# Rest rows of the first feed-forward product joined to the seven block products as prepared stacks

## The chip, the cores and the metric

The kernel runs on one core of one Trainium2 chip. The metric is device time in microseconds (us) of one execution. The engines are named as in the profile: PE (TensorE, matmuls), DVE (VectorE), ACT (ScalarE), POOL (GpSimd) and SP (SyncE, which issues most transfers); SPq and the like stand for the queue of instructions of an engine that only issues or waits.

## The reference

```python
x = A_x                                   # 1 x 2048 x 576
xn = layernorm(x)                         # no scale, no shift
qkv = xn @ wqkv                           # 32 heads of 18
phi = lambda t: where(t > 0, t + 1, exp(t)) + 1e-6
kv, z = sum over s of phi(k) v^T, phi(k)  # linear attention, not causal
o = (phi(q) @ kv) / (phi(q) . z + 1e-6)
s = o @ wo
h = gelu(xn @ w1 + b1)                    # w1: 576 x 4608
g = silu(h @ w2 + b2)                     # w2: 4608 x 576
out = x + s * g
```

## The kernel before

Every fp32 operand is split into a high and a low part (tiles ending in H and L, or h and l), and a product takes three matmuls: high by high, low by high, high by low. On top of that the large products use a seven-product scheme for 2x2 blocks (Winograd's form of Strassen's): sums of blocks are formed beforehand, seven block products are taken, and the results are combined.

The program has three stages, laid end to end on TensorE.

1. Keys and values (0 to about 155 us). Tiles of x are loaded, normalised, transposed and split (`x_hi`, `x_lo`, `x_sum`, `s_hi`, `s_lo`) into xH, xL, xSH and xSL, and these are also stored to DRAM (`x_dram`), since only half of the rows of x lie in SBUF at a time. Each has 4 column blocks of 128 rows and so many k slots.
2. Queries (about 155 to 282 us). Ten rounds r, with base = (8 + r) x 14 steps. A round runs a `Proj` (the query projection of a pair of 128-row tiles: psum tiles a, b, z, e; line 363) and two `Attend` halves. Attend transposes the queries scaled by the denominator (`pbuf`, transposed by PE into `ptp`, line 877; the last 64 columns of `pbuf` are filled by an ACT copy, line 869), casts them into `th` and multiplies them by the weights `kw` and `kr` (line 909). `kr` are copies of `kw` moved by some partitions with SBUF-to-SBUF transfers (lines 837 and 840). Beside it run the reloads of x (line 345), loads and sums of blocks of w2 (`w2r`, `w2o`, lines 491 to 525), and the stores of s (`s_dram`).
3. The feed-forward part (282 to 1071 us, and a tail to 1103). Two halves of x, nine chunks c of 512 hidden units each. A chunk is two `Up` steps (n counts them, 36 in all) and seven `product` calls of 24 matmuls each into the accumulators `macc`. An Up computes the first product for 256 hidden units and 512 rows: seven block products in the order UP = (1, 6, 7, 5, 2, 3, 4), all by the matmul at line 1162 with 512 columns. In the first half the operands of w1 are formed from `w1raw` (class W1: sums `T` on POOL, casts `hi` on ACT, subtractions `lo` on DVE) and stored in DRAM as `op_*`; in the second half W1Loaded reads them back.

D = 576 is 4 x 128 + 64. The 64 rest rows are a fifth k slot (KT = 5) that holds the high parts in one half of the partitions and the low parts in the other. In an Up two rest matmuls are added to each of the products 5, 2, 3 and 4, so these have 8 matmuls and the products 1, 6 and 7 have 6.

The order of the work on DVE, ACT, POOL and PE is that of the program text: `in_order` chains the instructions of each engine, and `add(step, what)` with `at_step(step)` puts work into the text at a numbered step. SP issues in the order of the text too. Each transfer on SP's queue uses one of eight completion semaphores in turn and so waits for the eighth one before it. `stage` takes one of six buffers; the tag `stw` has two.

Of the kernel before, what the change touches and what calls it, by code (L numbers as in the profile page):

```python
# [24 lines left out]
KT = 5  # L25
NF = F // P
# [11 lines left out]
NSP = 14  # L38
Q_ORDER = [4, 5, 6, 7, 0, 1, 2, 3]
# [3 lines left out]
def linear_attention_gated_ffn(ctx, tc, x, wqkv, wo, w1, b1, w2, b2, out):  # L43
# [40 lines left out]
    def stage_w1(name):  # L84
        return w1r.tile([P, 2 * KT * P], F32, tag="stw", name=name)

# [19 lines left out]
    b2b = pers.tile([P, D], F32, name="b2b")  # L106
# [14 lines left out]
    w1_dram, w2_dram = {}, {}  # L121

# [362 lines left out]
    def w2_load(c, pool, tag):  # L485
        src = w2_blocks(c)
        if tag == "wa":
            tiles = [pool.tile([P, KT * 2 * P], F32, tag=tag, name=f"w2r{c}{r}") for r in range(2)]
            parts = [t[:, : 2 * D].rearrange("p (n a d) -> p n a d", n=2, a=2) for t in tiles]
            for r in range(2):  # L490
                nc.sync.dma_start(parts[r], src[:, r])
        else:
            t = pool.tile([P, CF * D], F32, tag=tag, name=f"w2r{c}")
            nc.sync.dma_start(t, w2[c])
# [78 lines left out]
    x_raw(0, 0)  # L573
    wkq.split_k(3, kt_raw(raw_k, 3), GP)
# [16 lines left out]
    x_raw(0, 1)  # L591
    for i in (3, 2, 1, 5, 4):
        x_sum(0, i, GP, xf(0, 1))
# [9 lines left out]
    x_raw(1, 0)  # L603
    x_lo(1, 0)
# [6 lines left out]
    x_hi(1, 1), x_lo_tmp(1), x_lo(1, 1)  # L611
# [21 lines left out]
    def plan_pair(p):  # L633
        base = p * NSP
        def prepare(q, s, at_stats, at_norm, at_t, at_lo):
            add(base + at_stats, x_stats, q, s)
            add(base + at_norm, x_norm, q, s)
            if at_t is not None:
                add(base + at_t, transpose_x, q, s)
                add(base + at_t, x_hi, q, s)  # L640
                if s == 0:
                    add(base + at_lo, x_raw, q, s)
                add(base + at_lo, x_lo, q, s)
# [9 lines left out]
        if p == 1:  # L653
# [9 lines left out]
            add(base + 2, x_raw, 2, 0)  # L663
            add(base + 2, x_lo, 2, 0)
            add(base + 5, transpose_x, 2, 1)
            add(base + 5, x_hi, 2, 1)
            add(base + 5, x_lo, 2, 1)
# [11 lines left out]
        else:  # L679
# [6 lines left out]
            if p + 1 < NPAIR:  # L686
                q = p + 1
                add(base, x_norm, q, 1)
                add(base + 3, transpose_x, q, 1)
                add(base + 3, x_hi, q, 1)  # L690
                sums(q, (4, 4, 4, 6, 5), 7, 10, DV)
                add(base + 4, x_lo, q, 1)
                add(base + 6, x_lo_tmp, q)
# [61 lines left out]
    nc.sync.dma_start(b2b, bass.AP(tensor=b2.tensor, offset=b2.offset, ap=[[0, P], [1, D]]))  # L755
# [134 lines left out]

    class Attend:

        def __init__(self, r, s):
            self.t = t = pair_tile(Q_ORDER[r], s)
# [46 lines left out]
    class W1:  # L941


        def __init__(self, n):
            self.n = n
            raw = stage_w1(f"w1raw{n}")
            nc.sync.dma_start(raw, w1[n % NP])
            r4 = raw.rearrange("p (n k c) -> p n k c", n=2, k=KT)
# [4 lines left out]
        def T(self, i):  # L953
# [4 lines left out]
            if i in (5, 6):  # L958
                src[i] = w1p.tile([P, 2, P], F32, tag=f"w1t{i}", name=f"w1t{i}", bufs=1)
# [27 lines left out]
        def rest(self, n):  # L987
            return [v[:, (4, 2)[n]] for v in self.ops["ab"[n]]]

    W1_K = {"a": KT, "b": 3, 4: 2, 5: 2, 6: 2, 7: 2}  # L990

    class W1Loaded(W1):


        def __init__(self, n):
            self.n, self.ops = n, {}
            two = w1r.tile([P, 2, 2, 2, P], F32R, tag="stw", name=f"w67_{n}")
            for i in ("a", 6, 7, 5, "b", 4):
# [6 lines left out]
                nc.sync.dma_start(t.bitcast(F32), w1_dram[n % NP, i])  # L1005

# [8 lines left out]
    for r in range(NPAIR + 2):  # L1015
# [118 lines left out]
    gp = ctx.enter_context(tc.tile_pool(name="gp", bufs=1, side="right", reuse_waits="tile"))  # L1134
    fr = ctx.enter_context(tc.tile_pool(name="fr", bufs=1, side="right", reuse_waits="tile"))
    fl = ctx.enter_context(tc.tile_pool(name="fl", bufs=1, reuse_waits="tile"))

    macc = fl.tile([P, QH, 5, HD], F32, name="macc")
    C11, C12, C21, C22, U1 = range(5)
    mid = xp.tile([P, KT, 512], F32, tag="mid", name="mid")  # L1140
    m1_sb, u1_sb, u2_sb = (mid[:, i, :] for i in range(3))

    class Up:


        def __init__(self, n, w, xs):
            self.p, self.w = n % NP, w
            self.xb, self.xr = xs
# [5 lines left out]
        def mm(self, ps, i, rest=None, first=True):  # L1154
# [4 lines left out]
            if rest:  # L1159
                seq += [(v, self.xr[rest[1]]) for v in self.w.rest(rest[0])]  # L1160
# [12 lines left out]
        def step(self, i):  # L1173
# [12 lines left out]
            elif i == 5:  # L1186
                self.mm(E, 5, (1, 1))
                tt(B, E, u2_sb, op=ADD)  # L1188
                self.gelu(1, 1, B)
            elif i == 2:  # L1190
                self.mm(A, 2, (0, 0), first=False)
                self.gelu(0, 0, A)
            elif i == 3:
                self.mm(E, 3, (1, 2), first=False)
                tt(E, E, u1_sb, op=ADD)
                self.gelu(1, 0, E)
            else:
                self.mm(Y, 4, (0, 1))
# [43 lines left out]
    class HOps:  # L1242
# [11 lines left out]
        def S(self, i, pr):  # L1254
# [12 lines left out]
            else:  # L1267
                src[7, pr] = mid[:, 3 + pr, :]
# [20 lines left out]
    BIAS = {2: 0, 7: 1, 3: 1, 4: 0}  # L1289
    MINUS = (3, 5, 6, 7)  # L1290

    def product(c, i, q2, hs, w, held):
# [15 lines left out]
        if c > 0 or i in (5, 6):  # L1308
# [4 lines left out]
        elif i in BIAS:  # L1313
            h = BIAS[i]
            bb = b2b[:, None, h * HD : (h + 1) * HD].to_broadcast([P, 2, HD])
            if i in MINUS:
                nc.vector.tensor_tensor(dst, bb, src, op=SUB)
            else:
                nc.vector.tensor_tensor(dst, src, bb, op=ADD)
# [10 lines left out]
    tails = {}  # L1330

    def load_xs(t):
        F = lambda v: v.bitcast(F32)
        if t < 2:
            raw = stage_w1(f"xs{t}")
            xt, s_t = raw[:, :D], raw[:, KT * P : KT * P + D]
        elif t < 4:
            tiles = op_tile(w1p, [KT, P], "wa", 2, f"xs{t}")[1]
            xt, s_t = (F(v).rearrange("p a b -> p (a b)")[:, :D] for v in tiles)
# [116 lines left out]
    def x_swap(k):  # L1456
        _, a, b = X_PARTS[k]
        nc.sync.dma_start(x_tiles[k].bitcast(F32), x_dram[1][:, :, a:b])
# [46 lines left out]
    n_chunks = 2 * NC  # L1505
    for step in range(n_chunks):
# [3 lines left out]
        h = HOps(c)  # L1510
        if half == 0:
# [11 lines left out]
        if half == 0 and c < NC - 1:  # L1523
            add(base + 0, make, W1, w1t, 2 * step + 2)
            add(base + 4, make, W1, w1t, 2 * step + 3)
            add(base + 4, lambda n=2 * step + 2: plan_w1(add, w1t[n], base, **P0))
# [14 lines left out]
        elif not plain:  # L1541
            add(base + (14 if half == 0 else 7), make, W1Loaded, w1t, 2 * step + 2)
            swap = half == 0
            add(base + (22 if swap else 14), make, W1Loaded, w1t, 2 * step + 3)
            if step + 2 < n_chunks:
# [6 lines left out]
        if not plain:  # L1552
            if half == 0 and c == NC - 1:
                for k, at in ((2, 12), (3, 12), (1, 13), (0, 13)):
                    add(base + at, x_swap, k)
                add(base + 25, silu_first, C11)
# [87 lines left out]
```

## Time and profile before

| | |
|---|---|
| median of 3 runs | 1103.23 us (1102.82 to 1103.42) |
| span of the profiled execution, which is also its own time | 1103.0 us |
| PE busy | 1093.0 us in 6924 matmuls and transposes |
| DVE, ACT, POOL busy | 798.1, 505.7, 455.0 us |
| DMA moved | 271.92 MB, mean 247 GB/s |
| one chunk of the feed-forward part | two Ups of 11.33 us and 22.39 us of `product` |

A row of the timeline gives start and length in us, the engine, the line, the operation with out<-in, the shape, and in brackets the idle time ahead of it with what ended it. A row of the waits gives who waited at which line for whom: total us, times, longest. A row of the windows gives, for a stretch of time, its length, the busy us (and instructions) of PE, PEld (weight loads), DVE, ACT and POOL, the granted clock of PE, the DMA share (of 16 DMA engines) and GB/s.

### The profile page before, as it was taken

To read this page: it belongs to the slowest core of one execution; us is meant where nothing else is said; L and a number is where in the kernel's file an instruction comes from. 1 tells how busy PE (TensorE), PEld (TensorE's weight loads), DVE (VectorE), ACT (ScalarE), POOL (GpSimd) and SP (SyncE) were. 2 spreads that over 40 slices of the span, in tenths; PEclk is the share of its full clock that TensorE was granted. 3 is DMA by queue.
4 is the path that set the end of the run, shared out by engine and by line. 5 is a ranking of instruction groups with operands and counts; after the bars stand their busy time and mean duration, and the time that the engine had idled before them with its cause. 6 is when DMAs were issued, how large, how long until landed. Compare 5 with 4: busy or idle time off the path is not lost.

```text
span 1103.0 us, 18746 instructions
## 1 busy us (share of the span) xinstructions
PE 1093.0 (99%) x6924; PEld 1015.7 (92%) x6924; DVE 798.1 (72%) x1246; ACT 505.7 (46%) x916; POOL 455.0 (41%) x417
## 2 busy tenths in 40 slices
PE   8999999999999999999999999999999999999997
PEld 8999999999898998988989989899898998988987
DVE  5777567777687888978888788657475574664776
ACT  6766555545545444454444544524223233242352
POOL 5854434655446254453553633413324133342310
PEclk9999999999999999999999999999999999999999
DMA  5888837785988779688696789978666666766243
GB/s 205 308 264 280 275 116 226 256 286 190 350 282 314 262 237 369 182 299 300 219 369 194 267 285 376 371 236 281 212 220 205 219 200 210 229 197 223 85 139 124
DMA packets 95531, 271.92 MB, mean 247 GB/s; under 512 B 10381, under 2 KB 21133, under 8 KB 93391
## 3 DMA queue, kind: packets, MB, share of 16 engines
q1 hardware_dynamic: 90543, 260.68, 66.7%
q0 software_dynamic: 4896, 10.03, 5.5%
q8 instruction: 55, 0.90, 0.3%
q14 instruction: 37, 0.30, 0.1%
HBM read 165.94 MB, written 100.01 MB: 241 GB/s over the span
## 4 chain that ended last, share of the span: by engine, by line
PE 93%; DVE 2%; ACT 2%; issue 1%; DMA 0%; POOL 0%; SPq 0%; DVEq 0%; POOLq 0%; ACTq 0%
PE pm L1302 35%; PE e L1162 12%; PE zy L1162 10%; PE a L1162 10%; PE ps_s L909 5%; PE pl L419 5%; PE b L1162 4%; PE e L363 3%; PE a L363 2%; PE z L363 2%; PE pd L1427 2%; PE ps_kva L472 1%; PE b L363 1%; PE ptp L877 1%; PE pt L284 1%
## 5 line engine op out<-in xcount | busy, mean ns | idle before, releaser
L936 ACT CAST h_h<-g 128x512 fp32r<-128x512 f32 x204 | 120.1, 621 | 139.8 <-PE pm L1302 138.8
L939 DVE TENSOR_TENSOR h_l<-g,h_h 128x512 fp32r<-128x512 f32 x204 | 158.2, 775 | 0.0
L1310 DVE TENSOR_TENSOR macc<-macc,pm 128x576 f32<-128x576 f32 x128 | 96.3, 752 | 36.9 <-PE pm L1302 36.1
L1162 PE MATMUL a<-xH,wa 128*128 128x512 f32 x360 | 117.1, 390 | 0.0
L1269 POOL TENSOR_TENSOR mid<-g 128x512 f32<-128x512 f32 x34 | 45.4, 1336 | 108.2 <-ACT g L1170 108.1
L1312 DVE TENSOR_TENSOR macc<-pm,macc 128x576 f32<-128x576 f32 x90 | 68.2, 758 | 25.3 <-PE pm L1302 24.4
L1170 ACT ACTIVATE g<-b,b1c 128x512 f32<-128x512 f32 x36 | 24.9, 690 | 124.0 <-DVE b L1188 124.0
L1162 PEld LDWEIGHTS a<-xH,wa 128*128 128x128 f32 x360 | 67.6, 188 | 13.6
L1162 PE MATMUL e<-xSH,wb 128*128 128x512 f32 x216 | 66.6, 390 | 0.1
L1179 ACT COPY mid<-a 128x512 f32<-128x512 f32 x36 | 21.2, 588 | 90.8 <-PE a L1162 90.8
L1263 POOL TENSOR_TENSOR g<-g 128x512 f32<-128x512 f32 x34 | 51.4, 1512 | 17.1 <-DVE h_l L939 15.4
L1398 POOL TENSOR_TENSOR fin1l<-fin1h,fin1l 128x288 f32<-128x288 f32 x8 | 6.5, 808 | 121.7 <-DVE macc L1310 42.0
L1266 POOL TENSOR_TENSOR g<-g 128x512 f32<-128x512 f32 x34 | 52.5, 1543 | 10.0 <-DVE h_l L939 6.9
L1162 PE MATMUL a<-xL,wa 128*128 128x512 f32 x144 | 56.2, 390 | 0.0
L1182 DVE TENSOR_TENSOR mid<-b,mid 128x512 f32<-128x512 f32 x36 | 24.7, 687 | 36.3 <-PE b L1162 34.9
L1162 PE MATMUL b<-xSH,w 128*128 128x512 f32 x144 | 50.2, 389 | 0.0
L1162 PE MATMUL zy<-xSH,w 128*128 128x512 f32 x144 | 50.2, 389 | 0.0
L1162 PE MATMUL e<-xSH,w 128*128 128x512 f32 x144 | 50.2, 389 | 0.0
L1162 PE MATMUL zy<-xH,w 128*128 128x512 f32 x144 | 50.2, 389 | 0.0
L961 POOL TENSOR_TENSOR w1t<-w1raw 128x256 f32<-128x256 f32 x18 | 13.7, 762 | 86.3 <-DMA w1raw<-w 40.7
L1162 PEld LDWEIGHTS e<-xSH,wb 128*128 128x128 f32 x216 | 40.5, 188 | 9.0 <-DVE b L1188 0.6
L1260 POOL TENSOR_TENSOR g<-g 128x512 f32<-128x512 f32 x34 | 46.4, 1364 | 2.7
(931 smaller groups left out, 3579.0 us busy)
## 6 DMA issues: line engine op xcount, KB each, us to landing
op<-w SPq DMA_DIRECT2D x72, 256.0 KB
w<-op SPq DMA_DIRECT2D x72, 256.0 KB
w1raw<-w SPq DMA_DIRECT2D x18, 640.0 KB
w2raw<-w SPq DMA_DIRECT2D x10, 1152.0 KB
op_a<-wa SPq DMA_DIRECT2D x18, 640.0 KB
wa<-op_a SPq DMA_DIRECT2D x18, 640.0 KB
op<-w2o SPq DMA_DIRECT2D x19, 576.0 KB
w2r<-w SPq DMA_DIRECT2D x6, 1152.0 KB
```

The source lines that it names most:

```text
L363: nc.tensor.matmul(ps, st, mv, start=first and n == 0, stop=n == len(seq) - 1, skip_group_check=True,)
L419: nc.tensor.matmul(self.ps[n], st, self.wk(hl, k, n), start=(i == 0), stop=(i == n_all - 1))
L909: nc.tensor.matmul(self.ps[h], st[:, k, :], w[:, k, h * HD : (h + 1) * HD], start=(i == 0), stop=(i == len(self.seq) - 1),)
L936: nc.scalar.copy(pair[0], src)
L939: eng.tensor_tensor(pair[1], src, pair[0].bitcast(F32), op=SUB)
L1162: nc.tensor.matmul(ps.rearrange("p (c j) -> p c j", c=4), st, mv, start=first and n == 0, stop=n == len(seq) - 1, skip_group_check=True,)
L1260: tt(src[5, pr], A(1, 1), A(1, 0), op=SUB)
L1263: tt(src[6, pr], src[5, pr], A(0, 0), op=ADD)
L1266: tt(src[3, pr], src[6, pr], A(0, 1), op=SUB)
L1302: nc.tensor.matmul(ps[:, q, :HD], hs[p][st][:, cs], m[:, p, :], start=(n == 0 and i not in CHAIN), stop=(n == len(seq) - 1), skip_group_ch ...
L1310: nc.vector.tensor_tensor(dst, dst, src, op=SUB)
L1312: nc.vector.tensor_tensor(dst, src, dst, op=ADD)
```

## The change

The rest rows get one matmul in each of the seven products, so 42 + 7 matmuls in an Up in place of 42 + 8. For that, the block sums of the 64 rest rows (32 of each half of D's rest, RW = 32) are formed beforehand, and each is laid as a stack of four 32-row parts, high and low parts in such an order that one matmul over 128 rows gives all their products.

- In stage 1, `x_rest` copies the raw rest rows of x to DRAM (`xr_dram`), 4 small transfers for a pair of tiles, and one ACT copy `xr` for seven of the pairs.
- In stage 2, rounds r = 1 to 7 each make one `Rest`: (0, x), (0 to 4, w), (1, x). At `base` its input `rs` (128x512) is loaded on SP. At base + 3 ACT casts 128x384 (`hi(0)`), DVE subtracts (`lo(0)`) and SP issues four stores of 192 KB. At base + 4 POOL forms four sums of 128x128. At base + 6 the same follows for 128x512 (`hi(1)`, `lo(1)`, four stores of 256 KB). The stacks lie in DRAM as `xe_dram` and `we_dram`.
- In stage 3, each Up loads its stack of weights `we` (128x896, 448 KB). The seven stacks of x lie in three slots of xH and xSH that held the old rest rows (`load_x_over`) and in a new tile `x_extra` (1 MB), loaded at the start and again between the halves.
- w1 is loaded without its fifth k slot: `w1raw` and the operand a have 512 KB in place of 640, b has 256 in place of 384.
- The bias b2 is no longer read by `product`: `load_bias` loads it at the start of each half, and `set_bias` fills four of the accumulators with it by ACT copies of 128x4x288.
- The stores of s from the rounds r > 5 are issued by ACT in place of SP, and some small tiles move to other places.

The two tables of order show what stands where. First ACT at round r = 1, before: `scr<-a` are the drain and the first activation of the projection, `pbuf` are the copies that fill the last columns, `th` the cast of the transposed queries.

```order
L806 CAST kw_h<-kw_2045 128x576
L375 COPY scr<-a_2110 128x288
L387 ACTIVATE scr<-a_2110,c_84 128x288
L869 COPY pbuf_2040<-pbuf_2040 128x64
L884 CAST th_2174<-ptp_2168 128x640
L869 COPY pbuf_2041<-pbuf_2041 128x64
L806 CAST kw_h<-kr_2062 128x576
```

And ACT at the same place after the change (`re0True` is the stack of x, `rs0True` its input):

```order
L827 CAST kw_h<-kw_2098 128x576
L390 COPY scr<-a_2163 128x288
L923 CAST re0True_2204<-rs0True 128x384
L402 ACTIVATE scr<-a_2163,c_84 128x288
L890 COPY pbuf_2093<-pbuf_2093 128x64
L905 CAST th_2240<-ptp_2234 128x640
L890 COPY pbuf_2094<-pbuf_2094 128x64
L923 CAST re0True_2255<-rs0True 128x512
L827 CAST kw_h<-kr_2115 128x576
```

The two casts of the stack now stand between the drain of a and the cast of `kr`, the first of them ahead of the copy into `pbuf`.

SP at rounds r = 1 and 2, before:

```order
L840 DMA kr_2080<-kw_2045 120x576
L837 DMA kr_2080<-kw_2046 8x576
L345 DMA xL<-x_dram_100 128x768
L345 DMA xSH<-x_dram_100 128x1152
L345 DMA xSL<-x_dram_100 128x1024
L345 DMA xH<-x_dram_100 128x1024
L345 DMA xL<-x_dram_100 128x768
L491 DMA w2r_2219<-w 128x1152
L491 DMA w2r_2220<-w 128x1152
```

And after the change:

```order
L861 DMA kr_2133<-kw_2098 120x576
L858 DMA kr_2133<-kw_2099 8x576
L360 DMA xL<-x_dram_99 128x768
L360 DMA xSH<-x_dram_99 128x1152
L917 DMA rs0True<-xr_dram_102 128x512
L932 DMA xe_dram_104<-re0True_2204 128x384 x4
L932 DMA xe_dram_104<-re0True_2255 128x512 x4
L360 DMA xSL<-x_dram_99 128x1024
L360 DMA xH<-x_dram_99 128x1024
L360 DMA xL<-x_dram_99 128x768
L506 DMA w2r_2292<-w 128x1152
L506 DMA w2r_2293<-w 128x1152
```

The load of `rs` and the eight stores of the stacks stand ahead of the reload of xSL and of all that follows. The load of the next Rest stands behind the last of these rows.

SP at the start of stage 3, before (s is a store of the last Attend halves, `op` are stored operands of w1):

```order
L933 DMA op_5_3496<-w_0_3493 128x512
L918 DMA s_dram<-s_3528 128x576
L933 DMA op_b<-wb_3532 128x768
L933 DMA op_4_3540<-w_0_3537 128x512
L933 DMA op_a<-wa_3582 128x1280
L947 DMA w1raw_3587<-w 128x1280
```

And after the change (`we` are the stacks of weights for the first two Ups):

```order
L1217 DMA x_extra<-xe_dram_104 128x4x512
L985 DMA op_6_3680<-w_0_3677 128x512
L985 DMA op_7_3685<-w_0_3682 128x512
L985 DMA op_5_3690<-w_0_3687 128x512
L985 DMA op_b<-wb_3726 128x512
L985 DMA op_4_3734<-w_0_3731 128x512
L1044 DMA we_3758<-we_dram_106 128x896
L1044 DMA we_3760<-we_dram_106 128x896
L1235 DMA b2b<-b 128x576
```

The loads of `we` and b2b stand behind the stores of the last operands of the first Up, and `x_extra` ahead of four of them.

The diff, cut to its core:

```diff
+    def x_rest(p, s):
+        if s and p:
+            src = t1.tile([2 * RW, P], F32, tag="xr", name=f"xr{p}")
+            nc.scalar.copy(src, pts[p, 1][: 2 * RW, 4])
+        else:
+            src = xf(p, s)[: 2 * RW, 4]
+        dst = xr_dram[p // 4].rearrange("(r c) k j -> r c k j", c=4)[:, pair_cols(p)]
+        for k, at in enumerate(((0, 1), (3, 2))[s]):
+            nc.sync.dma_start(dst[:, at], src[k * RW : (k + 1) * RW])
...
+    class Rest:
+        def __init__(self, i, of_x=False):
+            self.i, self.of_x = i, of_x
+            self.s = stage(4 * P, f"rs{i}{of_x}").rearrange("p (k c) -> p k c", k=4)
+            nc.sync.dma_start(self.s, xr_dram[i] if of_x else w1e[i].rearrange("p (k c) -> p k c", k=4))
+        def hi(self, g):
+            n = (3, 4)[g]
+            t = w1r.tile([P, 2, 4, P], F32R, tag="stw", name=f"re{self.i}{self.of_x}{g}")
+            self.t = t[:, :, :n]
+            nc.scalar.copy(self.t[:, 0], self.s[:, :n])
+        def lo(self, g):
+            t, n = self.t, (3, 4)[g]
+            nc.vector.tensor_tensor(t[:, 1], self.s[:, :n], t[:, 0].bitcast(F32), op=SUB)
+            at = slice(3 * g, 3 * g + n)
+            for j in range(4):
+                v = t[:, j % 2 if self.of_x else j // 2].bitcast(F32)
+                dst = (xe_dram if self.of_x else we_dram)[self.i][RW * j : RW * (j + 1)]
+                nc.sync.dma_start(dst.rearrange("r c i j -> (r c) i j")[:, at], v)
+        def sums(self):
+            a, b, c, d = (self.s[:, k] for k in range(4))
+            tt = nc.gpsimd.tensor_tensor
+            if self.of_x:
+                tt(d, a, d, op=SUB), tt(c, c, d, op=SUB), tt(a, c, a, op=ADD), tt(b, b, c, op=SUB)
+            else:
+                tt(a, d, a, op=SUB), tt(d, c, d, op=SUB), tt(c, c, a, op=SUB), tt(b, b, c, op=SUB)
...
-            nc.sync.dma_start(s_dram[self.t], s_sb)
+            (nc.scalar if self.r > 5 else nc.sync).dma_start(s_dram[self.t], s_sb)
...
+        def load_rest(self):
+            n = self.n % NP
+            self.re = xe.tile([P, 7, P], F32R, tag="we", name=f"we{self.n}", bufs=2)
+            nc.sync.dma_start(self.re.bitcast(F32), we_dram[n // 4][:, n % 4])
...
+        if 1 <= r < NPAIR:
+            cur["re"] = None
+            i, of_x = ((0, True), (0, False), (1, False), (2, False), (3, False), (4, False), (1, True))[r - 1]
+            add(base, lambda i=i, of_x=of_x: cur.update(re=Rest(i, of_x)))
+            for g, at in ((0, 3), (1, 6)):
+                add(base + at, lambda g=g: cur["re"].hi(g))
+                add(base + at, lambda g=g: cur["re"].lo(g))
+            add(base + 4, lambda: cur["re"].sums())
+        if r == NPAIR - 1:
+            add(base + 8, load_x_over, 0)
...
+    load_x_extra(0)
+    for n in range(2):
+        w1t[n].load_rest()
...
+    def set_bias(s):
+        h = int(s in (C12, C22))
+        nc.scalar.copy(macc[:, :, s, :], tails["b2"][:, h : h + 1].to_broadcast([P, QH, HD]))
...
-            if rest:
-                seq += [(v, self.xr[rest[1]]) for v in self.w.rest(rest[0])]
+            seq += [(self.w.rest(i), xrest[i])]
...
+        if c == 0:
+            if half:
+                add(base + 2, load_bias)
+            for k, m in enumerate((C11, C22, C12, C21)):
+                add(base + (9 if half else 1) + k, set_bias, m)
```

More of the change, by code (lines that the diff above doesn't have):

```diff
@@ L25 @@
 KT = 5
+KM = 4
+RW = 32
 NF = F // P
@@ L121, in linear_attention_gated_ffn @@
     w1_dram, w2_dram = {}, {}
+    xr_dram = [dram.tile([P, 4, P], F32, name=f"xr_dram{i}") for i in range(2)]
+    xe_dram = [dram.tile([P, 4, 7, P], F32, name=f"xe_dram{i}") for i in range(2)]
+    we_dram = [dram.tile([P, 4, 7, P], F32, name=f"we_dram{i}") for i in range(NB4)]
     def x_operands():
@@ L487, in w2_load @@
         if tag == "wa":
-            tiles = [pool.tile([P, KT * 2 * P], F32, tag=tag, name=f"w2r{c}{r}") for r in range(2)]
-            parts = [t[:, : 2 * D].rearrange("p (n a d) -> p n a d", n=2, a=2) for t in tiles]
+            tiles = [pool.tile([P, 2 * D], F32, tag=tag, name=f"w2r{c}{r}") for r in range(2)]
+            parts = [t.rearrange("p (n a d) -> p n a d", n=2, a=2) for t in tiles]
             for r in range(2):
@@ L603, in linear_attention_gated_ffn @@
     x_raw(1, 0)
+    x_rest(1, 0)
     x_lo(1, 0)
@@ L1005, in __init__, with load_x_over @@
                 nc.sync.dma_start(t.bitcast(F32), w1_dram[n % NP, i])
+    X_OVER = {1: (xSH, 8, 0), 2: (xH, 7, 1), 4: (xH, 4, 2)}
+    X_EXTRA = (5, 3, 6, 7)
+    W_REST = {1: 0, 2: 1, 3: 2, 5: 3, 4: 4, 6: 5, 7: 6}
+    def load_x_over(i, which=(1, 2, 4)):
+        for k in which:
+            t, at, src = X_OVER[k]
+            nc.sync.dma_start(t[:, at].bitcast(F32), xe_dram[i][:, :, src])
     EW1 = nc.gpsimd
@@ L1544, in linear_attention_gated_ffn @@
             add(base + (22 if swap else 14), make, W1Loaded, w1t, 2 * step + 3)
+            for j in (2, 3):
+                add(base + (7, 14, 22)[j - 2 + swap], lambda n=2 * step + j: w1t[n].load_rest())
             if step + 2 < n_chunks:
```

101 lines of the change are left out of this document (63 added, 38 removed).

## The prediction

> **What bounds the kernel now.** I read the page first, then what TensorE waited for, then the chain that ended last, then the queues of SyncE and ScalarE around the places where the change adds work. The page:
>
> ```profile
> span 1103.0 us, 18746 instructions
> PE 1093.0 (99%) x6924; PEld 1015.7 (92%) x6924; DVE 798.1 (72%) x1246; ACT 505.7 (46%) x916; POOL 455.0 (41%) x417
> ```
>
> TensorE is busy for 99% of the span. What it waited for, first and last of six rows:
>
> ```profile
> PE warm L461 <- POOL ident masks.py:199: 1.7, 1, 1.7
> ...
> PE pt L284 <- DVE scr L324: 0.3, 1, 0.3
> ```
>
> No other wait of TensorE is longer than 0.6 us. So removed matmuls count in full, but every microsecond that TensorE is newly made to wait counts in full too; there is no slack on it. The chain of work (start, length, what) through a steady chunk gives the price of a matmul:
>
> ```profile
> 305.26 22.39 PE pm L1302 x168
> ...
> 329.04 1.37 PE b L1162 x6
> ...
> 331.77 1.81 PE e L1162 x8
> ```
>
> Products with 6 and with 8 matmuls stand side by side: 1.37/6 = 0.228, 1.81/8 = 0.226 us for one.
>
> **The gain.** An Up goes from 3x6 + 4x8 = 50 matmuls to 7x7 = 49. 36 Ups x 1 x 0.2265 us = **-8.2 us**, all on the path. The Trainium skill, "TensorE: Matmul & The Clock Gate", section "Back-to-back issue gap", gives some 131 ns as the sustained spacing of 512-wide matmuls; by that figure the gain would be an estimated 4.7 us. The rows disagree.
>
> **The cost at r=1 (the first Rest).** Rest(0, x) loads `rs` on SyncE's queue, and ScalarE casts it in `hi(0)`. In the new order that cast stands right behind `COPY scr<-a` and ahead of `ACTIVATE scr<-a,c`, of the pad `COPY pbuf` and of `CAST th` (the order is shown above). Its load takes the place that the reload of xSL had. Before, ScalarE's rows there are:
>
> ```profile
> 167.42 0.40 ACT L375 COPY scr<-a 128x288 f32<-128x288 f32 x1
> 171.04 0.50 ACT L387 ACTIVATE scr<-a,c 128x288 f32<-128x288 f32 x1 [3.23 <-PE a L363]
> 171.44 0.24 ACT L869 COPY pbuf<-pbuf 128x64 f32<-128x64 f32 x1
> 172.65 0.69 ACT L884 CAST th<-ptp 128x640 fp32r<-128x640 f32 x1 [0.97 <-PE ptp L877]
> ...
> 179.53 0.68 ACT L806 CAST kw_h<-kr 128x576 fp32r<-128x576 f32 x1 [0.63 <-DMA kr<-kw]
> 180.47 0.68 ACT L806 CAST kw_h<-kr 128x576 fp32r<-128x576 f32 x1 [0.26 <-DMA kr<-kw]
> ```
>
> SyncE's rows:
>
> ```profile
> 167.81 0.83 SPq L840 DMA_DIRECT2D kr<-kw  x1
> 168.74 0.67 SPq L837 DMA_DIRECT2D kr<-kw  x1
> 169.47 1.68 SPq L345 DMA_DIRECT2D xL<-x_dram  x1
> 171.21 0.41 SPq L345 DMA_DIRECT2D xSH<-x_dram  x1
> 171.67 0.65 SPq L345 DMA_DIRECT2D xSL<-x_dram  x1
> ...
> 191.99 0.40 SPq L494 DMA_DIRECT2D w2r<-w  x1
> ...
> 284.18 0.38 SPq L933 DMA_DIRECT2D op<-w  x1
> ```
>
> The shift copies `kr<-kw` issued at 165.8 to 168.7 release ScalarE only at 179.5 and 180.5, some 11 us after their issue. In windows (us; busy time of the five engines; granted clock; DMA share; GB/s):
>
> ```profile
> 10.00:15.00 5.00, 4.87 (x26) 4.80 (x26) 2.70 (x4) 3.09 (x8) 2.18 (x3) 0.66 1.04 391
> 160.00:172.00 12.00, 12.00 (x69) 9.54 (x68) 9.08 (x20) 6.64 (x15) 4.09 (x4) 1.00 0.24 56
> 176.00:178.00 2.00, 2.00 (x17) 1.99 (x16) 1.54 (x3) 1.84 (x4) 0.58 (x1) 1.00 1.03 312
> 178.00:180.00 2.00, 2.00 (x16) 1.85 (x14) 1.85 (x5) 1.37 (x3) 1.88 (x2) 1.00 0.59 192
> 182.00:184.00 2.00, 2.00 (x17) 2.00 (x17) 1.93 (x5) 0.00 (x0) 0.62 (x1) 1.00 1.02 419
> 182.00:265.00 83.00, 83.00 (x636) 83.00 (x636) 63.16 (x106) 43.80 (x89) 48.16 (x34) 1.00 0.66 238
> 282.00:304.00 22.00, 21.86 (x97) 17.75 (x97) 16.42 (x24) 14.31 (x27) 10.14 (x11) 1.00 0.97 340
> 663.00:688.00 25.00, 25.00 (x180) 24.50 (x179) 20.02 (x28) 10.45 (x16) 6.75 (x6) 1.00 0.96 373
> ```
>
> The queue runs dry until 172 (share 0.24), then is full while the copies are stuck in it, with a dip at 178 to 180. I take the queue as served in the order of issue: the last copy is done at 180.3, behind it xL (0.39 MB), xSH (0.59 MB) and the new load (0.26 MB), 1.24 MB at 419 GB/s = 3.0 us, so `rs` is there at 183.3. Then cast, ACTIVATE 0.50 and pad 0.24. The cast has 128x384 elements; rows of such size:
>
> ```profile
> L294 ACT CAST xH<-pt 128x384 fp32r<-128x384 f32 x8 | 3.8, 481 | 18.1 <-PE pt L284 18.1
> L327 ACT CAST xSH<-scr 128x1152 fp32r<-128x1152 f32 x8 | 9.2, 1145 | 1.5 <-POOL scr L324 1.5
> ```
>
> so the pad is ready at 183.3 + 0.48 + 0.50 + 0.24 less overlaps, about 184.4. The transposes `ptp` that read it start in these rows of TensorE:
>
> ```profile
> 171.90 0.71 PE L877 MATMUL ptp<-ident,pbuf 128*128 128x128 f32 x5
> ...
> 185.03 0.71 PE L877 MATMUL ptp<-ident,pbuf 128*128 128x128 f32 x5
> ...
> 200.21 0.71 PE L877 MATMUL ptp<-ident,pbuf 128*128 128x128 f32 x5
> ...
> 283.35 0.39 PE L1162 MATMUL b<-xSH,w 128*128 128x512 f32 x1
> ```
>
> 171.90 becomes 184.3: **+12.4 us**. Bounds: 5 us, if the load is only held up by bytes (rival 2), and 14 us.
>
> **r=2.** SyncE is in program order: eight stores of r=1's stacks (1.84 MB, the first ones only after the late cast), xSL, xH, xL (1.44 MB), two w2r (1.18 MB), then `rs` of Rest(0, w) (0.26 MB): 4.7 MB behind 183.8, 12.6 us at between 340 and 419 GB/s, so 196.4. The cast of it stands on ScalarE ahead of `ACTIVATE rt<-a,c`, and `lo(0)` stands on VectorE ahead of the last `kw_l<-kr`:
>
> ```profile
> 181.18 0.76 DVE L809 TENSOR_TENSOR kw_l<-kr,kw_h 128x576 fp32r<-128x576 f32 x1 [0.16 <-ACT kw_h L806]
> ```
>
> From that to the `ptp` at 185.03 were 3.85 us. 196.4 + 0.5 (cast) + 0.5 (lo) + 3.85 = 201.25, 16.2 us later than before: **+3.8 us** over r=1's. Bounds 0 and 6.
>
> **r=3 to r=6.** Each Rest moves 1.84 MB of stores and 0.26 MB of load in a period of 15.2 us (185.03 to 200.21), 138 GB/s on top of 238 at share 0.66; together 376 GB/s, a share of 1.04. The queue is full then. At r=3 `rs` is issued behind the w2r of 191.99 and its pad has to be cast some 1.2 us ahead of the `ptp` at 200.21, 6.6 us later. Ahead of it and in flight are w2r, xH and s (2.0 MB), with itself 5.4 us at 419 GB/s, in time; with the 1.84 MB of r=2's stores 9.8 us, 3.2 late. Between 0 and 3.2 for each of four, I take 2.0, since the stores of the step before are not all drained: **+8 us** (0 to 13). At r=7 only s and two `op` stores are ahead: 0.
>
> **What lies beside.** ScalarE's and VectorE's own work of Rest (casts of 0.48 and about 0.6, subtractions the same) and GpSimd's four sums hide in their idle time (VectorE 63 of 83 us, GpSimd 48 of 83). So do the `xr` copies and small stores of the first phase: TensorE's waits there are the six rows, and the x tiles wait for nothing of it. The last four stores of s on ScalarE's queue: 0. The smaller w1 loads and stores against the new `we` loads: +64 KB for an Up in the first half, 0.2 us of a queue: 0.
>
> **Start of the FFN.** we0 (0.46 MB) stands on SyncE behind `op_4`, which waits for VectorE and was issued at 284.18, and is read by the seventh matmul of the first Up, in the place of the row at 283.35. At 340 GB/s (share 0.97) its own bytes give 284.6 + 1.4 = 286.0, 2.6 us late; with x_extra (1.05 MB) and the six stores (1.8 MB) still ahead 11 us. I take **+5.5 us**, since part of these has left by then. The bias: four copies of 128x1152, 1.15 us each by the row of that size, on ScalarE, which wait for b2b behind we1. The chain there was already tight:
>
> ```profile
> 300.67 0.62 DVE b L1188
> 301.29 0.04 issue
> 301.33 2.11 PE e L1162 x8
> ```
>
> Between 0 (idle time of ScalarE, 7.7 of 22 us) and 4.6: **+2 us**. The exchange of x in the middle: 35 slots of 0.26 MB in place of 31, over a queue at share 0.96: 0 to 3, I take 0, since xL and the first half of xH now come with the same bytes ahead of them.
>
> **Clock.** The only long idle times of before are at the start; behind them a window of 5 us had 0.66 of the clock, 1.7 us lost. One stall of 12 us: **+1.5 us** (0 to 3).
>
> Sum: -8.2 + 12.4 + 3.8 + 8 + 5.5 + 2 + 1.5 = +25.0, against the profiled execution's 1103.0: **1128 us** (the median of the runs shown is 1103.23, 0.2 above it). A measurement of this kernel can tell 0.2%, 2.2 us, from no change.
>
> **Rivals.** 1. The forecast, 1119 to 1137 by its bounds taken together: 0.57.
> 2. The load passes the shift copies. Only bytes hold it up: 1.24 MB at 312 GB/s from 171.7 is 175.7, pad at 176.9, stall 5.0 in place of 12.4: 1121 us. For it: the dip at 178 to 180 shows that not all DMA engines are held by the copies. Against it: a load over 128 partitions needs all of them, and ScalarE saw the copies done in the order of their issue. 0.12. The Trainium skill, "DMA: Bandwidth & Descriptors", section "Queues, rings and completion order", speaks for it: completion is not first in, first out for an issuing engine; but each DMA engine takes descriptors in ring order, which speaks against it.
> 3. Only r=1 and r=2 cost: while TensorE stands 16 us the queue drains, and later loads are in time. -8.2 + 16.2 + 1.5 and 0 to 5 for the FFN's start: 1113 to 1118. 0.12.
> 4. Faster. `rs` lands before 171, so no cast holds the pad; then -8.2 and little else: 1095. It decides at the issue of that load: SyncE would have to be past xSH by about 168, while its rows show it held by the copies until 171.2. 0.10, for what I may have misread of the order.
> 5. The queue is full into the FFN: x_over, x_extra, we0, we1 and b2b are 3.5 MB, less 0.6 saved, 8.5 us at 340 GB/s, and w2's blocks are late for the products at 305; with 3 in the middle 1140. 0.06.
> Within 0.2%: between 4 and 3, 0.03.
>
> The range 1109 to 1142 leaves out rival 4, the no-change case and a few per cent at each end.
>
> **What would show it.** TensorE's `ptp` of r=1 with a wait of some 12 us put down to ScalarE's `pbuf`, and ScalarE's `re` cast waiting for the DMA `rs`; the same, smaller, at r=2 to 6; TensorE's first `L1262` row waiting for the DMA `we`; rows of seven matmuls at 1.59 us; the first Up starting at about 308 and the FFN from there to the end 8 us shorter. It is wrong if the wait of `rs` on ScalarE is under 2 us at r=1, or if the matmul spacing changes.

## The result, and the profile after

The changed kernel takes 1170.75 us (median of 5, 1167.0 to 1171.9), against 1103.33 us before: a ratio of 1.060 (95% interval 1.0588 to 1.0616). It is slower, as forecast, but by 67 us in place of 25. The profiled execution has a span of 1165.3 us, one of the faster ones. The page begins:

```profile
span 1165.3 us, 19017 instructions
PE 1106.0 (95%) x6888; PEld 1019.9 (88%) x6888; DVE 803.5 (69%) x1260; ACT 514.9 (44%) x945; POOL 461.9 (40%) x445
```

The 62.3 us between the spans split in two: TensorE's idle time went from 1103.0 - 1093.0 = 10.0 us to 1165.3 - 1106.0 = 59.3 us (+49.3), and its busy time rose by 13.0 us although 36 matmuls are gone. What TensorE waited for, the longest eight:

```profile
PE ptp L898 <- ACT pbuf L890: 20.4, 5, 11.3
PE a L1262 <- DMA we<-we_dram: 9.4, 1, 9.4
PE ptp L898 <- DVE th L910: 7.2, 4, 2.5
PE ps_s L961 <- DVE kw_l L830: 4.2, 1, 4.2
PE pm L1401 <- ACT h_h L988: 2.3, 1, 2.3
PE e L1262 <- DVE b L1288: 2.3, 1, 2.3
PE ptp L898 <- POOL pbuf L881: 1.8, 2, 1.0
PE warm L476 <- POOL ident masks.py:199: 1.7, 1, 1.7
```

Before, the last of these was the longest. ScalarE's own waits name what is behind the first row, the inputs of the Rests:

```profile
ACT re0True L923 <- DMA rs0True<-xr_dram: 14.9, 1, 14.9
...
ACT re3False L923 <- DMA rs3False<-w1e: 11.8, 1, 11.8
ACT re2False L923 <- DMA rs2False<-w1e: 11.6, 1, 11.6
ACT re4False L923 <- DMA rs4False<-w1e: 10.6, 1, 10.6
...
ACT re1False L923 <- DMA rs1False<-w1e: 8.6, 1, 8.6
...
ACT re0False L923 <- DMA rs0False<-w1e: 7.4, 1, 7.4
ACT re1True L923 <- DMA rs1True<-xr_dram: 6.3, 1, 6.3
```

All seven rounds are there. Round r = 1 on ScalarE reads as the prediction had it, cast, activation, pad, one behind the other:

```profile
181.31 0.51 ACT L923 CAST re0True<-rs0True 128x384 fp32r<-128x384 f32 x1 [14.89 <-DMA rs0True<-xr_dram]
181.72 0.49 ACT L402 ACTIVATE scr<-a,c 128x288 f32<-128x288 f32 x1
182.12 0.23 ACT L890 COPY pbuf<-pbuf 128x64 f32<-128x64 f32 x1
```

The later rounds, the start of the feed-forward part and the middle, on the chain that ended last:

```profile
190.12 7.98 DMA rs0False<-w1e
...
212.19 8.04 DMA rs1False<-w1e
...
235.47 7.33 DMA rs2False<-w1e
...
334.44 6.08 DMA we<-we_dram
...
757.62 9.29 DMA b2b<-b
...
797.19 1.62 PE a L1262 x7
800.42 1.61 PE zy L1262 x7
```

Each of these loads was needed about as soon as it was issued, or before, and each took 6 to 9 us to land.

**The clock.** Windows of the changed kernel around the first long wait (columns as before):

```profile
174.00:182.00 8.00, 0.00 (x0) 0.00 (x0) 0.15 (x1) 0.69 (x2) 0.45 (x1) 0.50 0.29 87
182.00:187.00 5.00, 4.60 (x21) 4.58 (x21) 3.92 (x8) 3.83 (x8) 1.33 (x3) 0.50 0.61 228
187.00:190.00 3.00, 3.00 (x25) 3.00 (x24) 2.42 (x6) 2.73 (x5) 1.76 (x2) 0.99 1.03 318
200.70:207.50 6.80, 5.94 (x27) 5.60 (x26) 4.37 (x10) 3.23 (x8) 4.07 (x6) 0.50 0.38 138
```

TensorE works again from 182.4, but at half its clock until 187, so 4.6 busy microseconds do the work of 2.3. At 200.7 the same follows a wait of only 4.2 us, and costs 3.0. The Trainium skill, "TensorE: Matmul & The Clock Gate", section "What's actually happening", has the clock halved after an idle window of some 3.4 us and restored after a busy one. The rows agree in part: the seven stretches at half clock last 3.4, 6.8, 10.2 or 13.7 us, multiples of that window, but the one from 200.7 was restored only after 6.8 us, 5.9 of them busy. Waits of 3.1 and 3.3 us in rounds 4 and 5 were enough here, and so were two of the four of 2.3 to 2.5 us.

### The profile page after: what moved, and what is told of

It reads as the page before. It is cut to its first block, busy times and chain, and to the rows that moved or that the text cites. A ratio compares the mean times of both kernels' runs of the same rounds, so it can differ in the third digit from the quotient of the medians.

```text
span 1165.3 us, 19017 instructions
## 1 busy us (share of the span) xinstructions
PE 1106.0 (95%) x6888; PEld 1019.9 (88%) x6888; DVE 803.5 (69%) x1260; ACT 514.9 (44%) x945; POOL 461.9 (40%) x445
## 4 chain that ended last, share of the span: by engine, by line
PE 79%; DMA 8%; DVE 4%; ACT 4%; issue 2%; POOL 2%; SPq 1%; DVEq 0%; ACTq 0%; POOLq 0%
PE pm L1401 33%; PE zy L1262 9%; PE e L1262 9%; PE a L1262 9%; PE b L1262 5%; PE pl L434 4%; PE pd L1516 2%; PE e L378 2%; PE a L378 1%; PE z L378 1%; PE ps_kva L487 1%; DMA rs0True<-xr_dram 1%; DMA b2b<-b 1%; DMA rs1False<-w1e 1%; DMA rs0False<-w1e 1%
## 5 line engine op out<-in xcount | busy, mean ns | idle before, releaser
L1409 DVE TENSOR_TENSOR macc<-macc,pm 128x576 f32<-128x576 f32 x136 | 102.2, 752 | 39.5 <-PE pm L1401 39.4
L1262 PE MATMUL a<-xH,wa 128*128 128x512 f32 x288 | 101.4, 393 | 0.0
L1411 DVE TENSOR_TENSOR macc<-pm,macc 128x576 f32<-128x576 f32 x98 | 74.2, 757 | 23.5 <-PE pm L1401 22.0
L1262 PEld LDWEIGHTS a<-xH,wa 128*128 128x128 f32 x288 | 54.0, 188 | 11.3
L1363 POOL TENSOR_TENSOR g<-g 128x512 f32<-128x512 f32 x34 | 49.5, 1457 | 27.5 <-DVE h_l L991 26.1
L1262 PE MATMUL e<-xSH,wb 128*128 128x512 f32 x144 | 50.4, 391 | 2.4 <-DVE b L1288 2.3
L1262 PE MATMUL e<-xSH,w 128*128 128x512 f32 x144 | 50.4, 390 | 0.0
L1015 POOL TENSOR_TENSOR mid<-w1raw 128x256 f32<-128x256 f32 x17 | 14.1, 832 | 81.1 <-DMA w1raw<-w 41.5
L1270 ACT ACTIVATE g<-e,b1c 128x512 f32<-128x512 f32 x36 | 24.8, 689 | 42.7 <-DVE e L1295 42.7
```

What stands on the lines that cost most here:

```text
L1262: nc.tensor.matmul(ps.rearrange("p (c j) -> p c j", c=4), st, mv, start=first and n == 0, stop=n == len(seq) - 1, skip_group_check=True,)
L1270: nc.scalar.activation(g, ps, AF.Gelu_apprx_tanh, bias=b1c[:, f : f + 1])
L1363: tt(src[6, pr], src[5, pr], A(0, 0), op=ADD)
L1409: nc.vector.tensor_tensor(dst, dst, src, op=SUB)
L1411: nc.vector.tensor_tensor(dst, src, dst, op=ADD)
```

## The experiments

Each ratio is to the kernel before, on the same chip.

**e1: the casts at the end of the round.**

```diff
-            for g, at in ((0, 3), (1, 6)):
+            for g, at in ((0, 9), (1, 12)):
...
-            add(base + 4, lambda: cur["re"].sums())
+            add(base + 10, lambda: cur["re"].sums())
```

> Only the places of the Rest steps in a round move: casts and subtractions from base + 3 and base + 6 to base + 9 and base + 12, the sums from base + 4 to base + 10; the loads stay. Theory A (an in-order ScalarE is held at the cast by a load that takes some 8 us to land): the casts now stand behind the pad copies and the load has landed, so most of the 35 us of TensorE waits in the rounds and the half clock behind them go: 1115 to 1130 us. Rival B (2.1 MB more in each round is more than the queue carries): the rounds stay long whatever the place, over 1150 us.

1153.65 us, 1.0454 (1.0436 to 1.0471): 17 us better, so the place counts, but over 1150 us, which is rival B's number. From round 2 on the rounds stay long, 16.8 to 20.9 us from one `ptp` to the next, where they took 15.2. The wait on the pad is gone from TensorE's list, and others are in its place:

```profile
PE z L378 <- ACT s L969: 10.9, 4, 3.4
PE a L378 <- ACT scr L390: 8.9, 1, 8.9
```

The second is round 1 again. That round has no Attend halves, so its last step comes right behind its projection, and the cast moved there still waits for the load:

```profile
182.83 0.51 ACT L923 CAST re0True<-rs0True 128x384 fp32r<-128x384 f32 x1 [5.81 <-DMA rs0True<-xr_dram]
```

The place of the cast chooses which work waits behind it.

**e2: the last stores of s back on SyncE.**

```diff
-            (nc.scalar if self.r > 5 else nc.sync).dma_start(s_dram[self.t], s_sb)
+            nc.sync.dma_start(s_dram[self.t], s_sb)
```

> The last stores of s go back from ScalarE's queue to SyncE's, nothing else. Theory A (the first we load waits for the store of s that took 7.7 us on ScalarE's queue, since it takes that store's memory): the 9.4 us wait of the first Up shrinks by 3 to 5 us, 1165 to 1168 us. Rival B (the load is late because the queue is full): unchanged within 2 us, 1169 to 1173 us.

1170.26 us, 1.0598 (1.0582 to 1.0614): unchanged. TensorE's wait for we is 9.8 us. The chain after had shown `we` behind a store of s of 7.7 us, and that was the last of several late things, not the cause. Theory A fell.

**e3: the second load of b2b early.**

```diff
-            if half:
-                add(base + 2, load_bias)
...
                 add(base + 13, load_x_over, 1, (2, 4))
+                add(base + 2, load_bias)
```

> The second load of b2b is issued in the last chunk of the first half, ahead of the exchange of x, in place of behind the stores of the first half's results. Theory A (ScalarE is held at the bias copy by that load): the 2.5 us of TensorE waits in the first chunk of the second half and the 3.4 us at half clock behind them go, 1166 to 1168 us. Rival B (the four copies of 1.15 us themselves are what delays the casts): 1170 to 1172 us.

1166.38 us, 1.0565 (1.055 to 1.0581): 4.4 us better, theory A. The late load of b2b, which held ScalarE and with it the casts for the first product of the second half, was most of the loss in the middle.

**e4: without Rest.** The rounds make no stacks; the feed-forward part loads as many bytes from the stored x.

```diff
-            add(base, lambda i=i, of_x=of_x: cur.update(re=Rest(i, of_x)))
-            for g, at in ((0, 3), (1, 6)):
-                add(base + at, lambda g=g: cur["re"].hi(g))
-                add(base + at, lambda g=g: cur["re"].lo(g))
-            add(base + 4, lambda: cur["re"].sums())
...
-            nc.sync.dma_start(self.re.bitcast(F32), we_dram[n // 4][:, n % 4])
+            nc.sync.dma_start(self.re.bitcast(F32), x_dram[0][:, n % 4, n % 24 : n % 24 + 7])
```

> The seven Rest steps are left out of the rounds; the feed-forward part loads stacks of the same size from the stored x instead, so its rest products are not those of the reference. Theory A (the rounds lose their time to Rest alone, 35 us of waits and the half clock behind them; the feed-forward part has its own losses at its start and its middle): rounds as before, 1103 - 4 for the matmuls + 9 to 18 for the start and the middle, 1108 to 1118 us. Rival B (the losses at the start of the feed-forward part also come from Rest's backlog): 1099 to 1104 us.

1114.27 us, 1.0093 (1.0078 to 1.0108): theory A. Rest costs 1170.75 - 1114.27 = 56 us. There was no wait for we at the first Up either: the order put that load at 275.27, some 7 us ahead of its use, where the changed kernel issues it at 334.44, after the first matmul of the Up at 329.68. So that wait went with Rest, in part as rival B has it; whether by the backlog or by the load's place ahead of the last stores of `op` in SyncE's queue, this run does not tell. What is left is 10 us above before.

```profile
ACT macc L1234 <- DMA b2b<-b: 6.2, 1, 6.2
```

That row is ScalarE's longest wait of the first chunk.

**e5: e1 with buffers of their own for the stacks.** (`tag="stw"` in w1r becomes `tag="re"`, two buffers in t2.)

> e1 (casts at the end of a round, 1153.7 us), and the stacks' tiles get two buffers of their own in place of sharing two with w2's operands. Theory A (in e1 the rounds are held by a ring: a cast of one waits until the store of the other has left its buffer, and the stores wait in the queue): another 10 to 25 us go, 1128 to 1144 us. Rival B (the volume of the queue sets the rounds): 1149 to 1154 us.

1151.41 us, 1.0434 (1.0416 to 1.0451): 2 us from e1. The shared ring was not the matter in e1; the time is rival B's.

**e6: e5 with each stack stored once.**

```diff
-            for j in range(4):
-                v = t[:, j % 2 if self.of_x else j // 2].bitcast(F32)
+            for j in range(2):
+                v = t[:, j].bitcast(F32)
```

> e5, and each stack's high and low parts are stored once in place of twice (0.92 MB in place of 1.84 in a round); the copies are made by the loads, which take 2 or 4 transfers over part of the partitions in place of one. Theory A (buffers and places were the whole matter): like e5 within 3 us. Rival B (the volume matters: 15.2 us of a round carry some 5.5 MB at 360 GB/s, the rounds before had 3.6): 6 to 15 us faster than e5.

1152.73 us, 1.0445 (1.0429 to 1.046): no gain as a whole, theory A's number. But the first Up started at 307.3 in place of e5's 313.8, so the rounds did gain 6.5 us from the smaller volume, as rival B has it. It was given back in the feed-forward part, where the loads are now two to four transfers each: TensorE's waits for we grew from 8.2 to 13.7 us, and the first chunk of the second half from 50.4 to 56.3 us.

**e7: the loads half a round earlier, the casts where they were.**

```diff
-            add(base, lambda i=i, of_x=of_x: cur.update(re=Rest(i, of_x)))
...
+            add(base, lambda: cur.update(re=cur["next"]))
+            if r < NPAIR - 1:
+                add(base + 5, lambda v=of[r]: cur.update(next=Rest(*v)))
```

> The changed kernel with the casts where they were, but the loads of the Rests of rounds 2 to 7 are issued in the middle of the round before. Theory A (a load of some 8 us issued too late holds ScalarE, and nothing else): rounds 2 to 7 lose their waits, only round 1's 11 us and its clock stay: 1130 to 1140 us. Rival B (ring of buffers and volume): the waits turn to others, 1150 to 1168 us.

1149.2 us, 1.0416 (1.04 to 1.0431): 21.5 us better, 0.8 us below rival B's range and far above theory A's. The pad waits of rounds 3 to 6 (9.1 us) and round 2's wait for `kw_l` (4.2 us) are gone and round 1's is left; the half clock between 200 and 300 is gone too.

```profile
PE ptp L898 <- ACT pbuf L890: 11.2, 1, 11.2
PE a L1266 <- DMA we<-we_dram: 8.7, 1, 8.7
PE ptp L898 <- DVE th L910: 6.5, 6, 1.3
```

So late loads are a large part of the rounds, but not all.

**e9: all of it.** The first load goes ahead of the shift copies, with e7's early loads at base + 7, e6's single stores, own buffers for the inputs and the second cast, and e3's early b2b.

> The changed kernel with five edits together: the load of the first Rest issued ahead of the folding of wo (before the shift copies), each later one in the round before, casts at their old places; inputs rs and the second cast in buffers of their own; stacks stored once in place of twice; the second load of b2b early. Theory A (late loads, shared buffers and the backlog of the queue together make the losses of the rounds, and also the 9 us at the first Up): rounds within 1 to 2 us of before's 15.2, no 11 us wait in round 1, 1106 to 1116 us, like the kernel without Rest. Rival B (the engines' own work of Rest in their in-order chains costs 2 to 3 us in each round whatever the loads do): 1120 to 1135 us.

1144.87 us, 1.0373 (1.0356 to 1.0391): worse than either theory. Round 1's wait is gone (0.9 us on `scr`), but a round takes 17.6 us, where it took 15.2, with every input landed in time. A round of before, and one of e9:

```profile
245.72:260.90 15.18, 15.18 (x119) 15.18 (x117) 11.92 (x20) 7.89 (x16) 8.88 (x7) 1.00 0.31 120
257.72:275.33 17.61, 15.90 (x119) 15.23 (x118) 12.08 (x21) 8.51 (x18) 10.37 (x11) 1.00 0.54 201
```

TensorE idles there 1.7 us at a full clock and at a DMA share of 0.54, so neither clock nor queue is what holds it. The chain in that round has no TensorE in it:

```profile
258.58 0.47 POOL rs4False L941
...
259.60 0.77 ACT e L465
260.38 0.67 ACT scr L465
261.04 0.58 ACT s L970 x2
261.62 0.59 ACT th L905
...
267.46 0.55 issue
268.01 0.29 DVE th L910
```

Rest's own part of it:

```profile
256.98 2.06 POOL L941 TENSOR_TENSOR rs4False<-rs4False 128x128 f32<-128x128 f32 x4
259.08 0.62 ACT L924 CAST re4False<-rs4False 128x512 fp32r<-128x512 f32 x1 [3.16 <-POOL rs4False L941]
```

The second cast waits for GpSimd's sums, ScalarE's activations and `th` stand behind the cast, and TensorE's transposes wait for `th`. That is the mechanism of this run's rival, Rest's own work in the in-order chains, though the time is above its range too. The first cast still shares its two buffers with w2's operands and waits 2.4 to 3.9 us for the stores of `w2o` in rounds 5 to 7, but the chain does not pass through it. No run keeps the loads and leaves this work out, so the trace shows the chain and no experiment does. The rest of e9's loss is at the feed-forward part: 10.1 us of waits for we at its start, 2.9 us for we and 3.3 for xL in the middle, and a stretch of 10.2 us at half clock at each place.

**e10: e9 with the first bias copies at steps 9 to 12.**

> e9, and the four bias copies of the first chunk go from steps 1 to 4 to steps 9 to 12, as in the second half. Theory A (these copies wait on ScalarE for b2b, 6 us on its way, and push the first chunk's activations): 4 to 7 us faster than e9. Rival B (the loss there comes from transfers of w1 and w2 that are late): like e9 within 1 us.

1147.54 us, 1.0388 (1.0372 to 1.0403): not better. In e9 the first Up waits for we in any case.

**e11: e4 without the bias copies. e12: the changed kernel without them.** In both a column of b1 is added where b2 was before the change, and b2b is neither loaded nor copied.

```diff
+            bb = b1c[:, None, h : h + 1].to_broadcast([P, 2, HD])
-            for k, m in enumerate((C11, C22, C12, C21)):
-                add(base + (9 if half else 1) + k, set_bias, m)
```

> e4 (no Rest, 1114.3 us), and the bias copies and both loads of b2b are left out; the first chunk's sums add a column of b1 in their place on VectorE, as the kernel before added b2. Theory A (ScalarE held by b2b and the copies makes what e4 still loses at the start and the middle of the feed-forward part): 1099 to 1103 us. Rival B (late transfers of w1, w2 and x make it): 1110 to 1115 us.

> The changed kernel with Rest in place, and the bias copies and loads of b2b left out in the same way. Theory A (the losses add up: the bias costs what it costs without Rest, 10 to 14 us): 1156 to 1161 us. Rival B (behind Rest's backlog the first Up waits for we in any case, and the bias copies hide there): 1164 to 1171 us.

e11: 1100.34 us, 0.9969 (0.9958 to 0.9981), 13.9 us below e4 and 3.5 us below before: theory A. Without Rest and without the bias copies the new matmuls do gain, and this is all that they gain. e12: 1162.08 us, 1.0528 (1.051 to 1.0545), 8.7 us below the changed kernel, between the two theories. In its trace the middle loses its 4.6 us, but the first chunk, where TensorE still waits 9.2 us for we, is only 1.3 us shorter (57.4 against 58.7 us): there most of the bias hides behind that wait.

**s1, s3 to s7: why 36 matmuls fewer gave 3.8 us.** Two Ups take 22.49 us before, from the first matmul's start to the last's, and 22.28 after, in every undisturbed chunk. These are 99 and 97 spacings; 97 at the old 22.49 / 99 = 0.2272 us would be 22.04. Each of these runs reads only that time. s1 is the kernel before with one rest matmul per product on the old operands (7 per product, no stacks). s3 to s7 are e4 with: weights of the rest matmul from operand a (s3); its moving operand from a slot of xH (s4); s4 with padded weight tiles and without the load of `x_extra` (s5); s5 with the weights of s3 too, so that both operands are old (s6); s6 with the temporaries of the operand sums in tiles of their own (s7).

```diff
-            seq += [(self.w.rest(i), xrest[i])]
+            seq += [(self.ops["a"][0][:, 0], xH[:, 4])]      # s6
```

> The kernel before with one rest matmul in each of the seven products, on the old operands, so 49 matmuls in an Up and products of 7, with no stacks and no Rest; its rest terms are not those of the reference. Theory A (the matmuls stand 229 ns apart in place of 227 since the products have 7 in place of 6 or 8): an Up pair of 22.28 us as in the changed kernel, 3.8 us faster than before, 1099 to 1101 us. Rival B (the spacing comes from the stacks' tiles): 227 ns, 22.04 us, 8.2 us faster, 1095 to 1097 us.

> The kernel without Rest (e4), and the rest matmul takes its weights from the tile of operand a in place of the stack we, which is still loaded; its moving operand stays the stack of x. Only the steady matmul spacing is read. Theory A (reading the we tile as weights makes the stream slower): two Ups 22.04 to 22.1 us, 227 ns. Rival B (something else of the change, the places of the tiles for one, makes it slower): 22.28 us, 229 ns as in the changed kernel.

> The kernel without Rest (e4), and the rest matmul takes its moving operand from a slot of xH in all seven products in place of the stacks of x, with we as weights. Only the steady spacing is read. Theory A (the moving reads of x_extra are slower): 22.04 to 22.1 us for two Ups. Rival B: 22.28 us.

> s4 (no Rest, rest matmul on xH and we), without the tile x_extra, and with the tiles of the operands a and b given the spare k slot that they had before the change, so that the high and low parts lie 2560 and 1536 bytes apart in a partition in place of 2048 and 1024. Only the steady spacing is read. Theory A (the places of w1's operands set the spacing): 22.04 us for two Ups, 227 ns. Rival B (they do not): 22.25 to 22.3 us, 229 ns.

> s5 (no Rest, no x_extra, padded tiles, rest matmul on xH), and the rest matmul takes its weights from the tile of operand a too, so that no matmul reads we, which is still loaded. Only the steady spacing is read. Theory A (either of the stacks among a product's operands is enough to make the stream slower): 22.04 us for two Ups, as with the old operands in s1. Rival B (the places of other tiles make it): 22.25 to 22.3 us.

> s6, and the temporaries of w1's sums and the second sum of block 7 go back to tiles of their own, as before the change. Only the steady spacing is read. If s6 has 22.25 us and this 22.04, the shared tiles make the difference; if both have 22.25 or more, it is none of the edits tried, and stays open.

| | s1 | s3 | s4 | s5 | s6 | s7 |
|---|---|---|---|---|---|---|
| two Ups, us | 22.04 | 22.25 | 22.28 | 22.28 | 22.04 | 22.04 |

The spacing of s1 is rival B's. As a whole it takes 1098.88 us, 0.9957 (0.9942 to 0.9972), 4.7 us below before and not the 8.1 of 18 such chunks: an undisturbed chunk takes 44.65 us in place of 45.10, but the first takes 46.08 in place of 45.52 and the next three 44.9 to 45.0. No run asks why these stretch. The chain of s6, and of the changed kernel at a like place:

```profile
564.62 1.59 PE zy L1253 x7
566.21 1.59 PE e L1253 x7
567.79 1.59 PE a L1253 x7
```

```profile
481.63 1.61 PE zy L1262 x7
483.24 1.61 PE e L1262 x7
484.86 1.61 PE a L1262 x7
```

A product of 7 takes 1.59 us with the old operands and 1.61 with a stack as weights (s4, s5), and 1.59 or 1.61 with one as moving operand alone (s3); either brings nearly the whole difference. The number of matmuls is ruled out by s1; padding changes nothing (s5), and s6 is at 22.04 with the temporaries where they were (s7 the same). In the starts of single matmuls the spacing is 226 or 227 ns in s1, while in the changed kernel it swings between 224 and 236 ns for some matmuls after those that read a stack, as it also does for the first nine of two Ups in both. That the seventh matmul reads another tile than its neighbours is not enough: in s6 it takes its weights from operand a beside neighbours that take theirs from other tiles, at 22.04. Why a stack does this stays open.

## Why the prediction was off

The direction and the mechanism of rounds 1 and 2 came as worked out, the sum did not. The changed kernel is 17.5 us behind at the `ptp` of round 2, 47.7 at the first Up, 60.8 at the first product and 62.3 at the end. By the terms:

- **Gain**, -8.2: measured -3.8 (18 x 0.21). A smaller step that failed is the price, 0.2265 us for each of the other 49 as well: they became slower themselves, from 0.2272 to 22.28 / 97 = 0.2297 us. The prediction named this as a sign of being wrong, and its rows of seven at 1.59 us came at 1.61. With the old operands the spacing is as priced (s1), with the stacks the kernel gains 3.5 us (e11).
- **r=1**, +12.4: the wait is 11.3 us. The queue served the load behind the copies: in the trace's completion records the last copy lands at 178.3, xL at 179.2, xSH at 180.6 and `rs` at 181.3, in the order of issue. Rival 2 (1121 us) is out.
- **r=2**, +3.8: `ptp` stands at 202.52 in place of 185.03, 17.5 us late, where r=1 and r=2 together were forecast at 16.2. The wait for `kw_l`, behind `lo(0)` as worked out, is 4.2 us, and 0.9 is for `pbuf`. The half clock from 200.7 to 207.5 costs some 3 us, most of it behind this `ptp`.
- **r=3 to r=6**, +8, and r=7, 0: this is the step that failed most. From `ptp` of round 3, 19.8 us late (220.01 against 200.21), to the first Up, 47.7 us late (329.68 against 281.96), it is +28 us. What TensorE waited for in that stretch, the longest three:

```profile
PE ptp L898 <- ACT pbuf L890: 9.1, 4, 3.3
PE ptp L898 <- DVE th L910: 7.2, 4, 2.5
PE ptp L898 <- POOL pbuf L881: 1.0, 1, 1.0
```

The wait that I priced, that of the pad for `rs`, came to 9.1 us over the four rounds, near the 8. Two parts that I had at nothing were missing. The second cast, the sums and the subtractions, costed at nothing on the strength of idle time, stand in chains in which each engine waits for the next: `ptp` waits 7.2 us for `th` here, and e9 shows 2.4 us a round with all loads in time. And the clock was at half three times in this stretch (from 228.0, 245.1 and 265.5), with 12.8 us of TensorE's busy time in it, so 6.4 us lost. Smaller waits are 2.4 us, and 2.8 us of longer busy time at the full clock stay open. Late loads also bring on waits of other kinds and half clock: issued earlier (e7), they give 21.5 us over all rounds.

- **Start of the feed-forward part**, +5.5 and +2: 47.7 us late at the first Up, 60.8 at the first product (366.0 against 305.26), so +13. The wait for we is 9.4 us, near the upper bound of 11, and the clock behind it is at half until 344. TensorE waits 2.3 us more for `b`. The bias costs between 8.7 us (with Rest) and 13.9 (without) over both halves, so the middle's loss is in it; 2 stood for it.
- **Middle**, 0: the first chunk of the second half takes 49.5 us (747.55 to 797.02) against 44.9 for its neighbours, +4.6; with b2b early (e3) it is 46.1, without the bias (e12) 44.9.
- **Clock**, +1.5: the seven stretches at half clock hold 30.2 us of TensorE's busy time, so 15.1 us are lost; before had one such stretch, at its start, 1.7 lost. I priced one stall. Here all five waits of 3.1 us or more were followed by half clock, and two of the four of 2.3 to 2.5 us; in e1 one of 3.4 us was not.

Rival 3, later rounds in time since TensorE's lateness lets the queue drain, did not come: SyncE issues in order, and its next loads stand behind stores that wait for the late casts, the longest 4.2 to 10.7 us for each of the seven Rests. Rival 5 named the place where the queue was full, but the larger loss was in the rounds ahead of it.

## What to carry to other kernels

Before work is put on engines with idle time, look at where it stands in each engine's order and in SyncE's: a load issued in the step before its use costs its whole way through the queue, and work that passes from one in-order engine to the next and back costs its chain, not its busy time. On a kernel where TensorE never waits, price every new wait of some 3 us or more twice, once for the wait and once for the clock behind it. And when a change buys few matmuls, measure them first with their real operands; here all of the machinery was bought for 3.8 us.

## What the runs showed that was not expected

A steady stream of 128x512 matmuls runs 1% slower when one matmul in seven takes either operand from a stack (22.25 to 22.28 us against 22.04 for 98), and not when it takes both from old tiles (s1, s6). And a transfer on ScalarE's queue was no faster than on SyncE's: the store of s issued there at 326.74 took 7.7 us, with SyncE's transfers in flight, and putting it back changed nothing (e2).
